# One-bank key groups, half-run query units and a ring of four load buffers in a fused attention and gated-convolution kernel

## The chip, the cores and the metric

The kernel runs on one core of one Trainium2 chip. The metric is the device time of one execution in microseconds (us); lower is better.

## The reference

Linear attention with a Hedgehog feature map, followed by a gated linear unit whose gate is a causal convolution. B = 8 batches, H = 8 heads, 576 tokens, head width 64, 128 features, model width 512.

```python
def phi(x):
    proj = np.einsum('bhsd,df->bhsf', x, w_phi)
    proj = proj - np.max(np.abs(proj), axis=-1, keepdims=True)
    return np.concatenate([np.exp(proj), np.exp(-proj)], axis=-1)
q_p, k_p = (phi(q), phi(k))
kv = np.einsum('bhsf,bhsd->bhfd', k_p, v)
z = np.sum(k_p, axis=2)
num = np.einsum('bhsf,bhfd->bhsd', q_p, kv)
den = np.einsum('bhsf,bhf->bhs', q_p, z)[..., None] + 1e-06
x = (num / den)                       # then heads are joined: B, S, 512
# gated unit, K = 5 taps
for k in range(K):
    gate_pre += conv_w[k][None, None, :] * xp[:, k:k + S, :]
gate = 1.0 / (1.0 + np.exp(-gate_pre))
out = (gate * (x @ w_val)) @ w_out
```

## The kernel before

The work is written as some 1,060 tasks, made by `build` and carried out by `Emit`. Each task has an engine and a place in the string ORDER, which was written out ahead of time; `Plan.follow` reads it, so every engine's instructions stand in the program in that order and each engine runs its own in sequence. FLEX names the engine (A ScalarE, D VectorE, P GpSimd) of each task that has a choice, and BANKS the PSUM banks of each group. There are eight banks, and a bank is used again only when everything that reads its group is done. WARM and ZERO place matmuls that compute nothing (zeros added to a group, or a product that nobody reads) at given places of the order.

A batch goes through these steps. All of k and q of a batch are 18 blocks of 128 columns, cut into `UNITS`: four units of four blocks and one of two.

- Loads. Batch 0 comes in float32 through SyncE's queue (`load32`), is transposed on TensorE (`tp32`) and copied out by `tc32`. Batches 1 to 7 come through GpSimd's queue as bf16 (`load`), from batch 2 on into two buffers KQN, one for k and one for q, and are transposed by DMA from SyncE's queue (`xpose`). `hold` and `holdx` are small GpSimd copies that hold later loads back until an earlier transfer is done.
- Keys. `kp` projects a unit into two PSUM banks (one for each half of the rows), VectorE takes the maxima over both banks at once (`kmax`, line 585), ScalarE the two exponentials, each over both banks (`kexp`, line 595). `ek` takes the exponentials of the maxima, `vs` multiplies v by them on GpSimd (line 610), and `st` sums the products of keys and values on TensorE (line 620); `kv` copies them out.
- Queries. `qm` projects and `qmax` takes maxima; the maxima are transposed (`mqt`), negated (`mqr`) and spread by `rx` (line 682); `qp` projects again and adds them in PSUM (lines 693 and 698), and `qexp` takes the exponentials (lines 706 and 709). In the units of `qp` the four blocks of a unit lie in both runs k of a head's columns of QTIL, a quarter of each.
- Numerators. `num` (line 719, and 726 for the remainder) waits for all query exponentials of the batch; `nrm` divides; the result is transposed on TensorE (`xtp`, line 748) and copied (`xtc`), or, for the batches in XB, transposed by DMA (`xtd`, line 755).
- Gated unit. `gate` (line 781), `tanh` (line 785), `val` (line 791), `gv` (line 797), `out` (lines 813 and 817), `oev` and the stores `odma`.

The order runs several batches at once: the keys of batch b+2 stand beside the queries of batch b+1 and the gated unit of batch b.

## Time and profile before

| | before |
|---|---|
| median of 3 runs | 218.91 us (218.59 to 219.14) |
| profiled execution | span 217.7 us; its own time is listed as no other figure, and the median lies 1.2 us above the span |
| busy: TensorE, ScalarE, VectorE, GpSimd | 195.5, 180.8, 170.2, 132.8 us |
| instructions | 9029 |
| DMA | 39.92 MB, mean 183 GB/s |

A group's row gives its line, engine and operation, what it writes and reads with its shape, the count, the busy time in us and the mean of one in ns, and then the idle time just before its instructions and what ended it. In the chain and in the order of time a row is start, duration, engine, line and how many instructions were merged. A bracket at the end is the idle time before it and its releaser. PEld is the loading of weights into TensorE, PEclk its granted clock.

### The profile page before, as it was taken

The page shows a single profiled execution, that of the slowest core. Times are in us where ns is not written, and L with a number is a line of the kernel's source. Part 1 is how long each engine was busy: PE and PEld are TensorE (multiplying, and loading weights), DVE is VectorE, ACT ScalarE, POOL GpSimd, SP SyncE. Part 2 cuts the span into 40 slices and gives each one's busy share as a digit, 9 for nine tenths or more (in the row PEclk, how much of TensorE's full clock was granted, in tenths as well). Part 3 has the DMA queues.
Part 4 walks back from the last instruction along what each step waited for, and adds up shares of the span by engine and source line. Part 5 has one row for each costly group of instructions (what it writes and reads, how often), then busy time and mean ns, then how long its engine had stood idle before and what let it go on. Part 6 is the DMA issues. An engine that isn't in the chain of part 4 may idle for free.

```text
span 217.7 us, 9029 instructions
## 1 busy us (share of the span) xinstructions
PE 195.5 (90%) x3946; PEld 138.6 (64%) x3946; DVE 170.2 (78%) x257; ACT 180.8 (83%) x267; POOL 132.8 (61%) x172
## 2 busy tenths in 40 slices
PE   2787887778999999998999999999999999899990
PEld 2555565566676676676857776567757766687740
DVE  3199979999789988997899978998699897654510
ACT  3589999999989899998999997999988988634251
POOL 3055999897793838970999089902993879210010
PEclk9999999999999999999999999999999999999997
DMA  6999998899899799989999778969953265764166
GB/s 177 364 234 215 302 188 231 149 174 199 144 152 284 139 135 213 302 154 174 233 276 168 88 165 248 190 142 203 287 183 89 63 160 128 81 168 97 48 186 202
DMA packets 49954, 39.92 MB, mean 183 GB/s; under 512 B 34165, under 2 KB 39541, under 8 KB 49914
## 3 DMA queue, kind: packets, MB, share of 16 engines
q1 hardware_dynamic: 43616, 28.65, 55.6%
q0 software_dynamic: 6032, 10.49, 26.3%
q8 instruction: 31, 0.51, 0.9%
q10 hardware_dynamic: 266, 0.21, 0.3%
q14 instruction: 9, 0.07, 0.1%
HBM read 30.48 MB, written 9.44 MB: 183 GB/s over the span
## 4 chain that ended last, share of the span: by engine, by line
PE 52%; ACT 23%; DVE 14%; DMA 5%; issue 4%; SPq 0%; DVEq 0%; ACTq 0%
PE PS L791 11%; ACT QTIL L706 9%; PE PS L781 9%; PE PS L813 9%; ACT KTIL L595 8%; DVE MQP L585 5%; PE PS L620 5%; PE PS L577 4%; PE PS L719 4%; DVE MK L585 3%; DMA KTIL<-in_k_dram 3%; PE PS L693 2%; DMA XT<-XN 2%; PE PS L817 2%; PE PS L698 2%
## 5 line engine op out<-in xcount | busy, mean ns | idle before, releaser
L595 ACT ACTIVATE KTIL<-PS 128x1024 bf16<-128x1024 f32 (+1 forms) x80 | 71.9, 960 | 4.1 <-PE PS L577 2.0
L610 POOL TENSOR_TENSOR VT<-VN,EK 128x1152 bf16<-128x1152 f32 x32 | 67.9, 2123 | 4.0 <-ACT EK L604 3.9
L706 ACT ACTIVATE QTIL<-PS 128x1024 bf16<-128x1024 f32 x64 | 62.5, 1044 | 2.4 <-PE PS L698 1.6
L682 POOL TENSOR_TENSOR RX<-MQR,ident 128x512 bf16<-128x512 bf16 (+1 forms) x39 | 36.6, 964 | 35.7 <-DVE MQR L670 26.0
L585 DVE TENSOR_REDUCE MK<-PS 128x8 f32<-128x1024 f32 (+1 forms) x40 | 44.2, 1112 | 2.9 <-PE PS L577 1.2
L585 DVE TENSOR_REDUCE MQP<-PS 128x8 bf16<-128x1024 f32 (+1 forms) x40 | 43.6, 1112 | 3.1 <-PE PS L577 2.3
L791 PE MATMUL PS<-XT,WV 128*128 128x288 bf16 x256 | 34.8, 286 | 0.3 <-DVE GV L797 0.2
L797 DVE SCALAR_TENSOR_TENSOR GV<-TH,PS 128x576 bf16<-128x576 bf16 x32 | 23.8, 752 | 10.4 <-PE PS L791 4.7
L813 PE MATMUL PS<-WOUT,GV 128*128 128x512 bf16 x128 | 31.3, 380 | 0.0
L791 PEld LDWEIGHTS <-WV 128*128 128x128 bf16 x256 | 23.8, 98 | 7.9 <-issue 1.4
L785 ACT ACTIVATE TH<-PS 128x576 bf16<-128x576 f32 x32 | 20.3, 663 | 9.5 <-PE PS L781 6.3
L620 PE MATMUL PS<-VT,KTIL 64*128 64x65 bf16 x1152 | 23.3, 191 | 1.1 <-issue 1.0
L781 PE MATMUL PS<-XT,GW 64*64 64x288 bf16 x640 | 23.1, 285 | 0.9 <-DMA XT<-XN 0.8
L740 DVE TENSOR_TENSOR XN<-PS,RCP 128x512 bf16<-128x512 f32 x32 | 22.1, 692 | 1.5 <-DMA XT<-XN 0.4
L620 PEld LDWEIGHTS <-KTIL 64*128 64x128 bf16 x1152 | 20.8, 94 | 3.8 <-issue 2.5
L719 PEld LDWEIGHTS <-QTIL 128*128 128x128 bf16 x512 | 18.3, 97 | 6.4 <-issue 4.0
L719 PE MATMUL PS<-KV,QTIL 128*128 128x65 bf16 x512 | 20.3, 194 | 0.3 <-DVE MQP L585 0.2
L781 PEld LDWEIGHTS <-GW 64*64 64x64 bf16 x640 | 17.8, 106 | 3.3 <-DVE RCP L737 0.9
L634 ACT ACTIVATE OUTS<-PS 128x512 f32<-128x512 f32 x22 | 13.5, 619 | 7.3 <-PE PS L813 6.1
L577 PE MATMUL PS<-W,qT 64*128 64x128 bf16 x288 | 15.1, 217 | 3.7 <-ACT qT L544 0.9
L813 PEld LDWEIGHTS <-GV 128*128 128x128 bf16 x128 | 11.1, 98 | 11.3 <-issue 0.6
L577 PEld LDWEIGHTS <-qT 64*128 64x128 bf16 x288 | 10.6, 94 | 10.3 <-issue 5.2
(79 smaller groups left out, 235.6 us busy)
## 6 DMA issues: line engine op xcount, KB each, us to landing
out_dram<-OUTS SPq DMA_DIRECT2D x32, 256.0 KB, 3.4
VN<-in_v_dram SPq DMA_DIRECT2D x7, 1152.0 KB, 6.3
KQN<-in_q_dram POOLq DMA_DIRECT2D x6, 576.0 KB, 8.3
KQN<-in_k_dram POOLq DMA_DIRECT2D x6, 576.0 KB, 9.8
KTIL<-in_k_dram SPq DMA_DIRECT2D x4, 288.0 KB, 4.5
VN<-in_v_dram POOLq DMA_DIRECT2D x1, 1152.0 KB, 10.6
KTIL<-in_q_dram SPq DMA_DIRECT2D x4, 256.0 KB, 5.7
out_dram<-OUTS SPq DMA_DIRECT2D x14, 64.0 KB, 2.6
```

The costliest lines, as they stand in the source:

```text
L577: nc.tensor.matmul(self.PS[:, t.grp.banks[par], i * P:(i + 1) * P], X[rows, (c0 + i) * P:(c0 + i + 1) * P], self.W2[rows, :], start=True, ...
L585: self.nc.vector.tensor_reduce(o, self.two(t.grp, n * P).rearrange("p a (c f) -> p a c f", f=F), AX.X, ALU.max, apply_absolute_value=True)
L595: self.nc.scalar.activation(self.KTIL[b % 2][:, s, c0:c0 + n, :, :].rearrange("p c a f -> p a c f"), self.two(t.grp, n * P).rearrange("p a ...
L610: nc.gpsimd.tensor_tensor(self.VT[g][:, s, :, 0:D], self.VN[b % 2][:, NC * g:NC * g + NC, :], e.to_broadcast([P, NC, D]), ALU.mult)
L620: nc.tensor.matmul(self.PS[:, t.grp.banks[ab], (s * 2 + x) * E1:(s * 2 + x + 1) * E1], self.KTIL[b % 2][rows, s, J // 2, J % 2, :], self.V ...
L682: self.nc.gpsimd.tensor_tensor(o, *wide(self.MQR[self.mq(b, u)][:, :], self.ident2), ALU.mult)
L706: self.nc.scalar.activation(o, i, AF.Exp, scale=1.0 - 2.0 * s)
L719: nc.tensor.matmul(self.PS[:, t.grp.banks[h // 4], (h % 4) * E1:(h % 4 + 1) * E1], Q[:, s, c % 2, h, (c // 2) * P:(c // 2 + 1) * P], self. ...
L781: self.nc.tensor.matmul(self.PS[o * D:(o + 1) * D, t.grp.banks[par], 0:R], self.GW[r, jj, 4 - m, :], X[r, 4 * a + jj, :, HALO - 8 * s:HALO ...
L791: self.nc.tensor.matmul(self.PS[:, t.grp.banks[par], 0:R], self.WV[:, i, (2 * j + par) * D:(2 * j + par + 2) * D], X[:, 4 * par + i, :, HA ...
L797: nc.vector.scalar_tensor_tensor(out=self.GV[b % 3][:, j, :, :], in0=self.TH[j][:, :, :], scalar=1.0, in1=self.two(t.grp, R), op0=ALU.add, ...
L813: nc.tensor.matmul(self.PS[:, t.grp.banks[0], :], GV[:, j, c % 2, (c // 2) * XH:(c // 2) * XH + P], self.WOUT[:, j, c % 2, :], start=(j == ...
```

## The change

Several things change at once, and ORDER, FLEX and BANKS are written anew (1,179 tasks).

- A key unit's two banks become two groups of one bank. `kp` still fills both; `kmax` and `kexp` work on one bank each, so there are twice as many of them at half the width, and each bank comes free by itself.
- `qp` units 0 to 3 now hold half of one run each: eight blocks' worth of rows, of one of the two runs. `num` c waits only for the two units of its run (or the remainder's one). `rx`, RX and the maxima follow that layout.
- Four KQN buffers in a ring; k is loaded before q; a load waits only for the transposition that read its buffer, and `holdx` is no longer called. GV has two buffers instead of three, OUTS six instead of eight.
- XB grows from batches 6 and 7 to 4, 5, 6 and 7.
- `rx` in all batches and `vs` may run on VectorE as well. By the new FLEX three `rx` (one before) and two `vs` (none before) do; ScalarE has 5 of batch 0's copies (9 before), 2 `kv` (4), 2 `xtc` (5) and 21 `oev` (22).
- w_phi comes in one DMA instead of two, the convolution weights through SyncE's queue. WARM and ZERO give 7 and 24 matmuls (6 and 152 before).

```diff
--- before.py
+++ after.py
-XB = (6, 7)
+QOF = {(0, 1): (0, 2), (2, 3, 4): (1, 3, 4), (0, 1, 2, 3, 4): (0, 1, 2, 3, 4)}
+QNEED = ((0, 1), (2, 3), (0, 1), (2, 3), (4,))
+XB = (4, 5, 6, 7)
 HOLDU = 4
-NO = 8
+NO = 6
+NK = 4
 NJ = 2 * NC
...
-WARM = (
-    "60:6:1 81:1:1 87:7:2 134:7:1 141:7:1 "
-)
-ZERO = "35:76:7 61:80:5 75:34:1 101:105:1 118:99:1 126:215:8 144:223:1 155:192:4 158:200:1 175:315:6 189:346:1 195:241:2 197:241:2 211:327:1"
+WARM = "97:7:4 111:2:2 277:6:1"
+ZERO = "171:215:6"
...
-                    hold = [None, A("lk", b, 0, "POOL", 0.15, fn("hold", HOLDU), [lds[HOLDU]], rank=-600)]
+                    hold = [None, A("lk", b, 0, "POOL", 0.15, fn("hold", HOLDU), lds + klds, rank=-600)]
+                else:
+                    klds = lds
...
-                hx = A("lk", b, 0, "POOL", 0.15, fn("holdx", b - 1), [G("xq", b - 1, 0)])
-                first = [hx]
+                first = [h["lk", b - 1]]
...
-            for w in "qk":
-                ld = A("l" + w, b, 0, "POOL", 0.75, fn("load", w, b), first, rank=-500 + (w == "k") if b == 1 else None, lat=0.6)
+            for w in "kq":
+                war = []
+                if b >= 2:
+                    n = 2 * b + "kq".index(w) - NK
+                    war = [G("x" + "kq"[n % 2], n // 2, 0)] if n >= 4 else []
+                ld = A("l" + w, b, 0, "POOL", 0.75, fn("load", w, b), first + war, rank=-500 + (w == "k") if b == 1 else None, lat=0.6)
                 xf[w] = A("l" + w, b, 0, "DMA", 4.2 if w == "k" else 3.9, None, [ld])
                 first = [ld]
+            h["lk", b] = ld
...
-                x = A("x" + w, b, 0, "SP", 2.7, fn("xpose", w, b), last + dp, lat=-1.5)
-                last = [x]
+                x = A("x" + w, b, 0, "SP", 2.7, fn("xpose", w, b), [xf[w]] + dp, lat=-1.5)
...
-            cc = A("mqt", 0, 0, "PE", 0.5, fn("c_cw"), [G("tp", "q", 1)], g, rank=-500)
+            cl = A("lk", 0, 0, "SP", 0.5, fn("c_cwl"), [])
+            cl = A("lk", 0, 0, "DMA", 3.0, None, [cl])
+            cc = A("mqt", 0, 0, "PE", 0.5, fn("c_cw"), [G("tp", "q", 1), cl], g, rank=-500)
...
         for u, (c0, n) in enumerate(UNITS):
-            g = plan.group("kp", 2)
-            kp = h["kp", b, u] = A("kp", b, u, "PE", 0.057 * n, fn("kp", b, u), [G("xk", b, u)], g, 1)
-            h["kmax", b, u] = A("kmax", b, u, "DVE", dve(2 * n * P, 0.08), fn("kmax", b, u), [kp, G("ek", b - 2)], g)
-            for s in range(2):
-                h["kexp", b, u, s] = A("kexp", b, u, "ACT", act(2 * n * P), fn("kexp", b, u, s),
-                                       [kp] + [G("st", b - 2, i, x) for i in range(2) for x in range(2)]
-                                       + ([G("tp", w, i) for i in range(NU) for w in "kq"] if b == 1 else []), g)
+            gs = [plan.group("kp", 1) for _ in range(2)]
+            kp = h["kp", b, u] = A("kp", b, u, "PE", 0.057 * n, fn("kp", b, u), [G("xk", b, u)], gs[0], 1, also=gs[1])
+            for a in range(2):
+                h["kmax", b, u, a] = A("kmax", b, u, "DVE", dve(n * P, 0.08), fn("kmax", b, u, a), [kp, G("ek", b - 2)], gs[a])
+                for s in range(2):
+                    h["kexp", b, u, s, a] = A("kexp", b, u, "ACT", act(n * P), fn("kexp", b, u, s, a),
+                                              [kp] + [G("st", b - 2, i, x) for i in range(2) for x in range(2)]
+                                              + ([G("tp", w, i) for i in range(NU) for w in "kq"] if b == 1 else []), gs[a])
...
-                h["vs", b, gi, s] = A("vs", b, gi, "POOL", 2.22, fn("vs", b, gi, s),
+                h["vs", b, gi, s] = A("vs", b, gi, ("POOL", "DVE"), (2.22, 1.36), fn("vs", b, gi, s),
                                       [eks[gi % len(eks)], G("lv", b)] + [G("st", b - 1, gi, x) for x in range(2)])
...
-            for u in us:
+            for u in QOF[us]:
                 n = UNITS[u][1]
-                h["rx", b, u] = A("rx", b, u, ("POOL", "DVE") if b == 0 else "POOL", (0.35 * n - 0.1, dve(n * P)) if b == 0 else 0.35 * n - 0.1,
+                h["rx", b, u] = A("rx", b, u, ("POOL", "DVE"), (0.35 * n - 0.1, dve(n * P)),
                                   fn("rx", b, u, i), [mqr, G("qp", b - 1, u)], gm if b == 0 else None)
...
-            qp = h["qp", b, u] = A("qp", b, u, "PE", 0.118 * n, fn("qp", b, u), [rx, G("xq", b, u)], g, 1)
+            qp = h["qp", b, u] = A("qp", b, u, "PE", 0.118 * n, fn("qp", b, u), [rx] + [G("xq", b, y) for y in QNEED[u]], g, 1)
...
-        allq = [G("qexp", b, u, s) for u in range(NU) for s in range(2)] + [G("kv", b, i) for i in range(2)]
         for c in range(5):
             g = plan.group("num", 2 if c < 4 else 1)
-            num = h["num", b, c] = A("num", b, c, "PE", 0.57 if c < 4 else 0.38, fn("num", b, c), allq,
+            need = [G("qexp", b, u, s) for u in ((2 * (c // 2), 2 * (c // 2) + 1) if c < 4 else (4,)) for s in range(2)]
+            num = h["num", b, c] = A("num", b, c, "PE", 0.57 if c < 4 else 0.38, fn("num", b, c), need + [G("kv", b, i) for i in range(2)],
...
-                              [h["tanh", b, j], vl] + [G("out", b - 3, c) for c in range(4)] + [G("gvc", b - 3)], g)
+                              [h["tanh", b, j], vl] + [G("out", b - 2, c) for c in range(4)] + [G("gvc", b - 2)], g)
...
-        bufs = TT("KQN", 2, [P, NC, 2 * D])
+        bufs = TT("KQN", NK, [P, NC, 2 * D])
         for b in range(2, B):
             for i, w in enumerate("kq"):
-                self.N[w][b] = bufs[i]
+                self.N[w][b] = bufs[(2 * b + i) % NK]
...
-        for i in range(2):
-            nc.scalar.dma_start(self.W32[i * D:(i + 1) * D, :], self.wphi[:, :])
+        nc.scalar.dma_start(self.W32[:, :], self.wphi[:, :].unsqueeze(0).to_broadcast([2, D, F]))
         nc.vector.tensor_copy(self.W2[:, :], self.W32[:, :])
-        nc.scalar.dma_start(self.cw5[:, :], self.wts[1][:, :])
+
+    def c_cwl(self, t):
+        self.nc.sync.dma_start(self.cw5[:, :], self.wts[1][:, :])
 
...
     def hold(self, t, u):
-        c = UNITS[u][0] * P
-        self.nc.gpsimd.tensor_copy(self.HOLD[:, :], self.XN32["q"][:, c:c + 1])
+        x = self.KTIL[1][:, :, :, :, :].rearrange("p s c a f -> p s (c a f)").bitcast(FP32)
+        self.nc.gpsimd.tensor_copy(self.HOLD[:, :, :], x.rearrange("p s (u x) -> p s u x", x=256)[:, :, :, 0])
...
+    def bank(self, t, par):
+        return t.grp.banks[par] if t.also is None else (t.grp, t.also)[par].banks[0]
...
-    def kmax(self, t, b, u):
+    def kps(self, t, n):
+        return self.PS[:, t.grp.banks[0], 0:n * P].rearrange("p (c f) -> p c f", f=F)
+
+    def kmax(self, t, b, u, a):
         c0, n = UNITS[u]
-        self.amax(t, self.MK[b % 2][:, c0:c0 + n, :].rearrange("p c a -> p a c"), n)
-
-    def kexp(self, t, b, u, s):
+        self.nc.vector.tensor_reduce(self.MK[b % 2][:, c0:c0 + n, a], self.kps(t, n), AX.X, ALU.max, apply_absolute_value=True)
+
+    def kexp(self, t, b, u, s, a):
         c0, n = UNITS[u]
-        self.nc.scalar.activation(
-            self.KTIL[b % 2][:, s, c0:c0 + n, :, :].rearrange("p c a f -> p a c f"),
-            self.two(t.grp, n * P).rearrange("p a (c f) -> p a c f", f=F),
-            AF.Exp, scale=1.0 - 2.0 * s)
+        self.nc.scalar.activation(self.KTIL[b % 2][:, s, c0:c0 + n, a, :], self.kps(t, n), AF.Exp, scale=1.0 - 2.0 * s)
 
...
-            nc.gpsimd.tensor_tensor(self.VT[g][:, s, :, 0:D], self.VN[b % 2][:, NC * g:NC * g + NC, :], e.to_broadcast([P, NC, D]), ALU.mult)
-            nc.gpsimd.tensor_copy(self.VT[g][:, s, :, D:E1], e)
+            eng = nc.gpsimd if t.eng == "POOL" else nc.vector
+            eng.tensor_tensor(self.VT[g][:, s, :, 0:D], self.VN[b % 2][:, NC * g:NC * g + NC, :], e.to_broadcast([P, NC, D]), ALU.mult)
+            eng.tensor_copy(self.VT[g][:, s, :, D:E1], e)
...
     def rx(self, t, b, u, i):
-        c0, n = UNITS[u]
+        y0, ny = self.qys(u)
+        nh = H if u < 4 else 2 * H
 
         def wide(m, e):
-            return (m.rearrange("p (h x) -> p h x", h=2 * H).unsqueeze(2).to_broadcast([P, 2 * H, n, 8]),
-                    e[:, c0:c0 + n].unsqueeze(1).unsqueeze(3).to_broadcast([P, 2 * H, n, 8]))
-
-        o = self.RX[u][:, :, 0:n, :]
+            m = m.rearrange("p (h k x) -> p h k x", h=H, k=2)[:, :, u // 2, :] if u < 4 else m.rearrange("p (h x) -> p h x", h=2 * H)
+            return (m.unsqueeze(2).to_broadcast([P, nh, ny, 8]),
+                    e[:, y0:y0 + ny].unsqueeze(1).unsqueeze(3).to_broadcast([P, nh, ny, 8]))
+
+        o = self.RX[u][:, 0:nh * ny * 8].rearrange("p (h y x) -> p h y x", h=nh, y=ny)
+        mq = self.mq(b, 2 if u in (1, 3) else 0 if u < 4 else 4)
         if t.eng == "POOL":
-            self.nc.gpsimd.tensor_tensor(o, *wide(self.MQR[self.mq(b, u)][:, :], self.ident2), ALU.mult)
-        else:
-            with self.nc.allow_low_precision("bf16 maxima"):
+            self.nc.gpsimd.tensor_tensor(o, *wide(self.MQR[mq][:, :], self.ident2), ALU.mult)
+            return
+        with self.nc.allow_low_precision("bf16 maxima"):
+            if b == 0:
                 self.nc.vector.tensor_tensor(o, *wide(self.PS[:, t.grp.banks[0], :].bitcast(BF16)[:, 0:P], self.nident2), ALU.mult)
+            else:
+                self.nc.vector.tensor_tensor(o, *wide(self.MQR[mq][:, :], self.ident2), ALU.mult)
+
+    def qys(self, u):
+        return (8 * (u % 2), 8) if u < 4 else UNITS[4]
 
     def qp(self, t, b, u):
         nc = self.nc
-        c0, n = UNITS[u]
+        y0, ny = self.qys(u)
+        w = UNITS[u][1] * P
...
-            nc.tensor.matmul(self.PS[:, t.grp.banks[par], 0:n * P], self.W2[rows, :],
-                             X[rows, c0 * P:(c0 + n) * P].rearrange("p (y h x) -> p h y x", y=n, h=2 * H),
+            m = X[rows, y0 * P:(y0 + ny) * P]
+            m = m.rearrange("p (y h k x) -> p h k y x", y=ny, h=H, k=2)[:, :, u // 2] if u < 4 else m.rearrange("p (y h x) -> p h y x", y=ny, h=2 * H)
+            nc.tensor.matmul(self.PS[:, t.grp.banks[par], 0:w], self.W2[rows, :], m,
                              start=True, stop=True, skip_group_check=True)
...
-            o = self.QTIL[b % 2][:, s, :, :, :].rearrange("p a h (k r) -> p a (h k) r", k=2)[:, :, :, u * 32:(u + 1) * 32]
-            self.nc.scalar.activation(o, i, AF.Exp, scale=1.0 - 2.0 * s)
+            self.nc.scalar.activation(self.QTIL[b % 2][:, s, :, :, u * D:(u + 1) * D],
+                                      self.two(t.grp, n * P).rearrange("p a (h r) -> p a h r", h=H), AF.Exp, scale=1.0 - 2.0 * s)
...
-        GV = self.GV[b % 3]
+        GV = self.GV[b % 2]
```

45 lines of the change are left out of this document (22 added, 23 removed), and 77 rows, old and new, of the table ORDER.

## The prediction

> **What bounds the kernel now.** The page comes first: its span, its busy shares, its slices and its chain.
>
> ```profile
> span 217.7 us, 9029 instructions
> ...
> PE 195.5 (90%) x3946; PEld 138.6 (64%) x3946; DVE 170.2 (78%) x257; ACT 180.8 (83%) x267; POOL 132.8 (61%) x172
> ...
> PE   2787887778999999998999999999999999899990
> DVE  3199979999789988997899978998699897654510
> ACT  3589999999989899998999997999988988634251
> ...
> PE 52%; ACT 23%; DVE 14%; DMA 5%; issue 4%; SPq 0%; DVEq 0%; ACTq 0%
> ```
>
> The span is 217.7 us; the median of the three timed runs is 218.91, so 1.2 us lie around the span, and every sum below is made against the span. TensorE is busy for 90%, yet its digits are 7 and 8 in the first ten slices and 9 almost everywhere behind. ScalarE and VectorE show the reverse: at 9 from the third slice on, falling off only at the end. The chain says the same: TensorE carries 52% of it, ScalarE 23% and VectorE 14%. So there are two stages, and the view of windows separates them.
>
> ```profile
> core 0: us, PE busy (x) PEld busy (x) DVE busy (x) ACT busy (x) POOL busy (x), PEclk, DMA share, GB/s
> 0.00:10.00 10.00, 4.93 (x32) 3.83 (x33) 2.00 (x6) 3.83 (x5) 1.78 (x12) 1.00 0.82 258
> 10.00:20.00 10.00, 7.73 (x122) 5.60 (x121) 9.32 (x10) 9.34 (x15) 5.68 (x8) 1.00 1.08 244
> 20.00:30.00 10.00, 8.39 (x136) 5.49 (x137) 8.45 (x15) 9.28 (x18) 8.13 (x7) 1.00 1.09 244
> 30.00:40.00 10.00, 8.45 (x272) 6.57 (x271) 9.57 (x12) 9.60 (x13) 9.19 (x12) 1.00 0.93 214
> 40.00:50.00 10.00, 7.38 (x202) 5.88 (x197) 8.94 (x16) 9.78 (x13) 9.97 (x10) 1.00 0.96 166
> 50.00:60.00 10.00, 9.28 (x225) 6.42 (x223) 8.46 (x12) 9.46 (x16) 7.12 (x10) 1.00 0.95 170
> 180.00:190.00 10.00, 9.61 (x266) 6.93 (x266) 6.94 (x16) 7.58 (x12) 6.12 (x8) 1.00 0.63 92
> ```
>
> From 10 to 50 us ScalarE is busy 38.0 of 40 us and VectorE 36.3, while TensorE has 32.0, part of it filler (below). There the exponentials and maxima set the pace, and TensorE waits for PSUM banks. From 50 us on TensorE is at 9.28 of 10 and more, and it stays there to the end. A change can therefore gain in three places: by getting through the first 50 us sooner, by taking matmuls away behind them, and by closing the gaps of the last 30 us. What it adds to ScalarE or VectorE costs most in the first stage.
>
> **The change part by part.** The groups with their shapes kept apart, and the order of the first 54 us, price the pieces.
>
> ```profile
> L595 ACT ACTIVATE KTIL<-PS 128x1024 bf16<-128x1024 f32 x64 | 63.5, 1050 | 2.6 <-DVE MK L585 1.3 <-PE PS L577 0.6 <-DVE GV L797 0.3
> L595 ACT ACTIVATE KTIL<-PS 128x512 bf16<-128x512 f32 x16 | 8.8, 602 | 1.5 <-PE PS L577 1.3
> L585 DVE TENSOR_REDUCE MK<-PS 128x8 f32<-128x1024 f32 x32 | 38.9, 1219 | 2.3 <-PE PS L577 1.2 <-ACT KTIL L595 0.7 <-ACT KV L632 0.2
> L585 DVE TENSOR_REDUCE MK<-PS 128x4 f32<-128x512 f32 x8 | 5.5, 686 | 0.7 <-ACT KTIL L595 0.3 <-PE PS L504 0.3
> L610 POOL TENSOR_TENSOR VT<-VN,EK 128x1152 bf16<-128x1152 f32 x32 | 67.9, 2123 | 4.0 <-ACT EK L604 3.9
> L632 ACT CAST KV<-PS 128x520 bf16<-128x520 f32 x4 | 2.5, 625 | 0.0
> L632 ACT COPY XT<-PS 128x1024 bf16<-128x1024 bf16 x2 | 2.1, 1043 | 0.0
> L504 PE MATMUL PS<-ONES,NIL 64*128 64x128 bf16 x140 | 5.6, 216 | 0.0
> ```
>
> ```profile
> 7.29 0.90 PE L536 MATMUL PS<-ident_f,KTIL 128*128 128x128 f32 x3 [1.21 <-DMA KTIL<-in_k_dram]
> 8.13 1.04 PE L577 MATMUL PS<-W,kT 64*128 64x128 bf16 x16
> 9.21 1.94 ACT L595 ACTIVATE KTIL<-PS 128x1024 bf16<-128x1024 f32 x2 [0.39 <-PE PS L577]
> 10.32 0.69 DVE L542 CAST qT<-PS 128x512 bf16<-128x512 f32 x1 [4.80 <-ACT KTIL L595]
> 10.93 2.35 DVE L585 TENSOR_REDUCE MK<-PS 128x8 f32<-128x1024 f32 x2
> 18.49 1.09 ACT L595 ACTIVATE KTIL<-PS 128x512 bf16<-128x512 f32 x2
> 28.23 0.63 PE L577 MATMUL PS<-W,qT 64*128 64x128 bf16 x16
> 53.85 1.28 ACT L785 ACTIVATE TH<-PS 128x576 bf16<-128x576 f32 x2
> ```
>
> *Splitting the key units.* Each batch has four units of 1024 columns and one of 512; each becomes two one-bank halves. So 40 maxima become 80 on VectorE and 80 exponentials become 160 on ScalarE. A pair of 1024-wide exponentials takes 1.94 from the first start to the last end; less one duration of 1.05 the second starts 0.89 after the first. A pair of 512-wide ones takes 1.09, less 0.60 is 0.49. Two halves cost 0.98 against 0.89: 0.09 per split, 80 x 0.09 = 7.2 us on ScalarE. From the means alone it would be 2 x 0.602 - 1.050 = 0.154 per split, 12.3 us; that is the upper bound, and zero the lower one, if the halves start while the other bank is still being filled or reduced. I take 0.09, because ScalarE runs these operations back to back in the crowded stages. On VectorE a pair of 1024-wide maxima takes 2.35, so the second starts 1.13 behind the first; a half takes 0.69, and with the same overlap of 0.09 0.60: 0.07 per split, 2.8 us in all.
>
> The errata section of the Trainium skill's page "VectorE: DVE Perf Modes" speaks against this part: it charges ScalarE 172 cycles per instruction that reads PSUM, and asks for tiles of 512 elements or more. At the 1.2 GHz it gives that is an estimated 0.143 per split, close to the upper bound and 11.5 us in all; the pair of halves at 18.49, 0.49 apart, does not bear that out for operations that follow one another.
>
> *Work moved between engines.* Decoding the letters of FLEX against the tasks: ScalarE loses 4 of its 9 first-batch copies, 2 of its 4 KV copies, one 1024-wide and two narrow XT copies and one output copy. At 0.49 per half-width operation, 0.9 for the wide one and 0.3 for a narrow one that is 7 x 0.49 + 0.9 + 0.6 = 4.9 us. VectorE takes the copies (4 + 2 + 1, at 0.60: 4.2), two of the 32 VT products and a net two of the RX products. No row shows a VT product on VectorE. GpSimd's 2.12 is the upper bound; the maxima's slope, (1219 - 686) / 512 = 1.04 ns per column, gives 1.2 plus overhead as the lower one. I take 1.5 with its small copy, since the slope is VectorE's own: 3.0; the RX products at the half's 0.60: 1.2. With the splits VectorE gains 2.8 + 4.2 + 3.0 + 1.2 = 11.2 us, XT copies left at nothing because it gets as many as it loses but for one.
>
> *The first stage.* Before, the third key transposition stood ahead of the first projection, waited 1.21 us for its load, and with that projection at 8.13 the first exponential came at 9.21. The new order has two key transpositions, a small query unit and then the projection. The wait of 1.21 and the 0.84 from 7.29 to 8.13 go; the small query load, now first on SyncE, gives back some 0.4: -1.7. VectorE, idle for 4.80 us until 10.32, now starts with the first copies. From the first exponential to the first tanh (53.85) ScalarE has two copies fewer (-1.0) and 26 splits (+2.3). That is -0.4 by ScalarE's work alone. Of its idle time, 2.0 us in 10 to 50, half closes, I estimate, since a numerator now needs only its own half of the query exponentials and VectorE is ahead: together -1.5. Bounds: -3.5 with its idle time all gone and splits at 0.05, +1.0 with none gone and VectorE late (its 4.80 us cover 2.4 of copies and 26 x 0.07 of splits, so there is room of 0.6 only).
>
> *Behind it.* XB sends the transpositions of batches 4 and 5 through DMA as well: four groups of TensorE transpositions less. The chain shows what one costs.
>
> ```profile
> 157.88 0.45 PE PS L748 x8
> 177.72 0.49 PE PS L719 x16
> 185.71 4.54 DMA XT<-XN
> 190.38 2.03 PE PS L781 x60
> 212.61 0.60 ACT OUTS L634
> ```
>
> 4 x 0.45 = -1.8 us of matmul time in the stage that TensorE bounds (0 where ScalarE has the end). Against it ScalarE has the other 54 splits, +4.9, less the 2.9 of KV, XT and output copies: +2.0. TensorE carries more than twice the chain that ScalarE does, so I put half of it on the path: +1.0. Bounds 0 and +3.1, that is all of it and 8 us of VectorE's additions at its 14% of the chain.
>
> *The end.* Gate matmuls of batch 6 begin at 190.38, when their DMA transposition has landed 4.54 us after the last normalization allowed it; from there TensorE is never out of work, and the last output copy begins at 212.61. The order of time gives TensorE's wait for it:
>
> ```profile
> 190.38 2.03 PE L781 MATMUL PS<-XT,GW 64*64 64x288 bf16 x60 [0.77 <-DMA XT<-XN]
> ```
>
> The new order puts two numerators (0.49 each) that stood behind that point ahead of it, and three output units of batch 5 there as cover. -0.8, bounds -1.8 (the two numerators and the wait) and +0.4. The last store is a whole 256 KB one:
>
> ```profile
> XT<-XN SPq DMA_TRANSPOSE x4, 3.8
> out_dram<-OUTS SPq DMA_DIRECT2D x32, 256.0 KB, 3.4
> ```
>
> Its 3.4 after an issue comes to what lies between 213.2 (212.61 + 0.60) and 217.7 now, so the tail of the tail stays.
>
> *Loads.* The ring of four lets k and q loads go ahead, and the copies that held GpSimd back are gone. The queue's own waits show what that is worth:
>
> ```profile
> SPq L565 <- DMA KQN<-in_k_dram: 49.8, 5, 19.7
> ```
>
> SyncE stood 49.8 us waiting for these loads, but the chain has no such load behind the first batch. This removes a wait that nobody waits for: 0. What I name as its cover is the order of SyncE's queue: stores and DMA transpositions stand behind those waits (rival two). GV falls to two buffers, OUTS to six: the products of batch b wait for the outputs of b-2, which stand ahead in TensorE's own order: 0. The convolution weights' load moves from ScalarE's queue to SyncE's, behind the first kT transposition; its reader stands behind the first numerators: 0, and up to +0.5 if SyncE is late. The run halves of the query units change patterns, not counts: 0.
>
> Sum: -1.5 - 1.8 - 0.8 + 1.0 = -3.1, so a span of 214.6 and, with 1.2 around it, **215.8 us**.
>
> **Rivals.** *One: the fixed cost per instruction wins.* Place: ScalarE, in both stages. If a split costs the 0.154 of the means, the first stage becomes +0.2 and the second 54 x 0.154 - 2.9 = +5.4, with ScalarE and no longer TensorE at the end of most waits, so that the 1.8 of transpositions is hidden: 0.2 + 5.4 - 0.8 = +4.8 if all of it is exposed, +2 if half is: 221 to 223.7, I say 222. It decides from about 0.15 per split on (3.1 / (26 + 27) above 0.09). For it: ScalarE at 9.3 to 9.8 of 10 in the first windows. Against: the spacing of 0.49. The errata rule quoted above would put the kernel just below that point, at about 218.6.
>
> *Two: the DMA transpositions of batches 4 and 5 arrive late.* Place: SyncE's queue, where they stand behind the kT transposition of batch 7, which waits for a load that GpSimd sends only after batch 5's RX products. One exposed transposition costs what the chain shows, 4.54, so 220.3. Against it: between the last numerator of batch 4 and its gate matmuls the order has four state, five numerator, four output, two value units, fifteen in all; each at no less than the 0.45 of the shortest row shown, that is 6.8 us at the least, against 4.54. It decides when SyncE reaches them more than 2.3 us late; the 49.8 us of waits say that SyncE can be late.
>
> *Three: nothing moves.* The first stage's gain is eaten by splits and the rest by an order that is tight elsewhere: 218.6 to 219.3, say 218.9.
>
> *Four: the clock.* The tables ZERO and WARM give 158 filler matmuls before and 31 after; the 5.6 us of L504 nearly vanish. In the first 10 us 16 projections took 1.04, at 28.23 0.63, though PEclk says 1.00 of both windows. If a quarter of the 26 us of real matmul time in 10 to 50 fell back to the first pace, 4.2 us more, three of them uncovered: 218.8 to 219. The Trainium skill's page "TensorE: Matmul & The Clock Gate", part 1, says that an idle window of some 3.4 us halves the clock. TensorE's longest wait in the rows shown is 1.21, so by that rule the clock stays and the forecast with it.
>
> **How the numbers follow.** The forecast has 0.50; the same with the first stage at its good end and the end at -1.8 (211.5 to 213) 0.10; rival one 0.14, two 0.11, three 0.10, four 0.05. About 0.3% (0.66 us) is what can be told from no change here. Faster by more than that: 0.60; within it: 0.10; slower: 0.30. The range leaves out the far ends of the good case and of rival one: 211.5 to 221.5. The likely side alone, the forecast with its bounds on the fast side, is 212.5 to 217.8.
>
> **What would show it.** Right: first exponential near 7.5 us; first tanh near 52; 512-wide KTIL exponentials about 0.49 apart; the group of XN transpositions down by 32 matmuls, with four more XT DMA transpositions; TensorE at 9 from the ninth slice; gate matmuls of batch 6 near 187. Wrong: halves 0.55 or more apart, or ScalarE at 10 of 10 with TensorE below 9 in the middle (one); idle time ahead of the gate group released by XT<-XN (two); a granted clock below 1 or 16 projections in 1 us after 10 us (four); a first tanh after 54 us would take my largest term away.

## The result and the profile after

The changed kernel takes 235.41 us (median of 4 runs, 234.2 to 240.32) where the kernel before took 218.88: a ratio of 1.0739 (95% interval 1.0687 to 1.0791), 16.2 us more. The forecast was 215.8. Ratios here and below leave out the runs that took over 1.5% more than the fastest of the same kernel. The page of the profiled run (235.77 us):

```profile
span 234.0 us, 8798 instructions
...
PE 198.8 (85%) x3770; PEld 138.0 (59%) x3787; DVE 180.8 (77%) x309; ACT 181.9 (78%) x337; POOL 127.2 (54%) x161
...
PE   2898698699999789869996999998699959799991
...
PEclk9999959999999999999999999999689999999999
...
q8 instruction: 29, 0.48, 0.8%
...
PE 56%; DVE 21%; DMA 9%; issue 6%; ACT 5%; POOL 1%; SPq 0%; DVEq 0%; POOLq 0%; ACTq 0%
```

TensorE's unbroken row of nines is gone: there are holes in the middle, and in two places the granted clock falls. DMA went from 5% of the chain to 9%, "issue" (time in which the engine waited for nothing that the profile shows) from 4% to 6%. The windows show part of the first stage and the two worst stretches:

```profile
core 0: us, PE busy (x) PEld busy (x) DVE busy (x) ACT busy (x) POOL busy (x), PEclk, DMA share, GB/s
...
30.00:40.00 10.00, 9.19 (x250) 7.78 (x247) 8.27 (x14) 9.60 (x20) 7.69 (x11) 0.73 0.99 143
40.00:50.00 10.00, 7.51 (x192) 6.01 (x186) 9.59 (x21) 9.71 (x18) 10.00 (x11) 1.00 1.17 194
50.00:60.00 10.00, 9.47 (x250) 6.88 (x244) 8.89 (x15) 9.53 (x20) 8.35 (x10) 1.00 1.14 157
160.00:170.00 10.00, 6.82 (x77) 3.99 (x69) 5.24 (x9) 4.17 (x9) 8.37 (x10) 0.75 0.86 209
180.00:190.00 10.00, 7.30 (x198) 5.40 (x198) 8.16 (x14) 7.30 (x12) 5.63 (x9) 1.00 0.77 245
```

In 160 to 170 us TensorE is idle for about a third of the time, VectorE and ScalarE for about a half: something outside them is late. TensorE's order of time has the five large holes behind the first stage (the bracket is the idle time before the row):

```profile
80.24 0.84 PE L638 MATMUL PS<-VT,KTIL 64*128 64x65 bf16 x42 [1.65 <-issue]
103.84 0.23 PE L638 MATMUL PS<-VT,KTIL 64*128 64x65 bf16 x4 [1.97 <-issue]
128.10 0.43 PE L810 MATMUL PS<-XT,GW 64*64 64x288 bf16 x6 [1.81 <-issue]
165.96 2.08 PE L820 MATMUL PS<-XT,WV 128*128 128x288 bf16 x8 [3.13 <-DVE OUTS L648]
189.76 0.82 PE L842 MATMUL PS<-WOUT,GV 128*128 128x512 bf16 x3 [2.70 <-issue]
```

Four of the five are "issue". The fourth has a named cause, VectorE's output copy, which itself waited for a store:

```profile
DVE OUTS L648 <- DMA out_dram<-OUTS: 3.9, 1, 3.9
...
PE PS L820 <- DVE OUTS L648: 3.1, 1, 3.1
```

The holes come to 11.3 us. Behind the fourth the clock was at half for 6.83 us (the trace's clock records: 165.07 to 171.90). TensorE ran again from 165.96, so this is worth at most 3.0 us of matmul time. Together that is 14.2 of the 16.3 us between the spans; whether each hole is lost time the sum doesn't say, the runs below do. Where the loss arises is seen when TensorE's work (columns streamed, a float32 one counted four times, without fillers and without the transpositions of XN) is laid against time (us), worked out from the matmuls of the traces. In the two profiles of the changed kernel 16 of the 128 matmuls of the output line have no record; they are counted in evenly with the rest of their line:

```
share done    before   changed   changed with few loads (below)
0.20           62.4      61.5      61.4
0.40          103.6     107.5     102.8
0.60          141.0     148.6     142.9
0.80          176.4     192.4     179.0
1.00          212.5     228.9     215.5
```

The changed kernel leads by 0.9 us at some 60 us and loses all of its time behind.

**What the "issue" holes are.** The page has a DMA queue of its own for instructions: q8, 29 packets, 0.48 MB, so 16 KB each. TensorE has 7,574 recorded instructions in this program, some 261 for each packet; a piece is taken here as 256 instructions, which the shifts of runs 5 to 7 test. The trace's DMA records give the start of each packet. Beside those of the four holes stand the large loads in flight (first and last packet, same records) and how many of TensorE's recorded instructions had run when it stopped, less 256 for each fetch made before:

```
fetch starts   large load in flight      hole at    instructions used up
 77.80         v, 74.2 to 78.2            78.6       440
101.40         v, 96.9 to 101.3          101.9       437
125.84         q, 122.4 to 125.8         126.3       436
187.52         v, 183.2 to 187.7         187.1       427
```

Each of the four fetches begins within some 0.4 us of the end of a load that has held the DMA engines for 3.4 to 4.5 us; TensorE goes on some 1.4 us after the packet has landed. 17 of TensorE's 7,574 records are missing in this trace; in the first experiment's, which has them all, the counts at its four such holes are 442, 442, 442 and 440. The earliest fetches in these traces start at a count of some 160. So TensorE can run to a count of 442, could be served from about 160 on, and stops when the fetch is late. Ahead of each of the four holes it ran groups of its short instructions, the 65-column states. Not every fetch waits for a load's end: those at 70.50, 83.53 and 137.31 began inside a load of q or k, at counts of 275, 345 and 238, and made no hole. In the kernel before the latest fetch starts at a count of 343, at 47.04, so TensorE never runs out there.

### The profile page after: what moved, and what is told of

Read it like the earlier page. It is cut to its first block, busy times and chain, and to the rows that moved or that the text cites. A ratio compares the mean times of both kernels' runs of the same rounds, so it can differ in the third digit from the quotient of the medians.

```text
span 234.0 us, 8798 instructions
## 1 busy us (share of the span) xinstructions
PE 198.8 (85%) x3770; PEld 138.0 (59%) x3787; DVE 180.8 (77%) x309; ACT 181.9 (78%) x337; POOL 127.2 (54%) x161
## 4 chain that ended last, share of the span: by engine, by line
PE 56%; DVE 21%; DMA 9%; issue 6%; ACT 5%; POOL 1%; SPq 0%; DVEq 0%; POOLq 0%; ACTq 0%
PE PS L820 11%; PE PS L842 11%; PE PS L810 7%; PE PS L591 6%; DVE MQP L602 6%; PE PS L638 6%; DVE MK L611 5%; PE PS L748 5%; DMA qT<-KQN 4%; DVE XN L769 3%; DMA out_dram<-OUTS 3%; PE PS L723 2%; DMA KTIL<-in_k_dram 2%; PE PS L846 2%; ACT KTIL L615 2%
## 5 line engine op out<-in xcount | busy, mean ns | idle before, releaser
L615 ACT ACTIVATE KTIL<-PS 128x512 bf16<-128x512 f32 (+1 forms) x160 | 80.4, 580 | 10.7 <-DVE MK L611 6.2
L628 POOL TENSOR_TENSOR VT<-VN,EK 128x1152 bf16<-128x1152 f32 x30 | 63.5, 2118 | 29.9 <-ACT EK L621 22.4
L733 ACT ACTIVATE QTIL<-PS 128x1024 bf16<-128x1024 f32 x64 | 64.6, 1043 | 5.3 <-PE PS L727 5.2
L611 DVE TENSOR_REDUCE MK<-PS 128x4 f32<-128x512 f32 (+1 forms) x80 | 48.3, 627 | 3.7 <-PE PS L591 2.3
L703 POOL TENSOR_TENSOR RX<-MQR,ident 128x512 bf16<-128x512 bf16 (+1 forms) x37 | 35.2, 973 | 26.6 <-DVE MQR L688 21.7
L820 PE MATMUL PS<-XT,WV 128*128 128x288 bf16 x256 | 36.1, 291 | 3.9 <-DVE OUTS L648 3.1
L842 PE MATMUL PS<-WOUT,GV 128*128 128x512 bf16 x112 | 30.2, 380 | 3.8 <-issue 3.2
L638 PEld LDWEIGHTS <-KTIL 64*128 64x128 bf16 x1152 | 21.8, 97 | 8.8 <-issue 4.8
L810 PE MATMUL PS<-XT,GW 64*64 64x288 bf16 x640 | 24.4, 290 | 2.0 <-issue 1.8
L652 ACT ACTIVATE OUTS<-PS 128x512 f32<-128x512 f32 x21 | 13.0, 619 | 15.1 <-PE PS L842 11.5
L591 PE MATMUL PS<-W,qT 64*128 64x128 bf16 x288 | 16.6, 230 | 3.9 <-DVE MQP L602 1.1
```

The source lines that it names most:

```text
L591: nc.tensor.matmul(self.PS[:, self.bank(t, par), i * P:(i + 1) * P], X[rows, (c0 + i) * P:(c0 + i + 1) * P], self.W2[rows, :], start=True, ...
L611: self.nc.vector.tensor_reduce(self.MK[b % 2][:, c0:c0 + n, a], self.kps(t, n), AX.X, ALU.max, apply_absolute_value=True)
L615: self.nc.scalar.activation(self.KTIL[b % 2][:, s, c0:c0 + n, a, :], self.kps(t, n), AF.Exp, scale=1.0 - 2.0 * s)
L628: eng.tensor_tensor(self.VT[g][:, s, :, 0:D], self.VN[b % 2][:, NC * g:NC * g + NC, :], e.to_broadcast([P, NC, D]), ALU.mult)
L638: nc.tensor.matmul(self.PS[:, t.grp.banks[ab], (s * 2 + x) * E1:(s * 2 + x + 1) * E1], self.KTIL[b % 2][rows, s, J // 2, J % 2, :], self.V ...
L703: self.nc.gpsimd.tensor_tensor(o, *wide(self.MQR[mq][:, :], self.ident2), ALU.mult)
```

## The experiments

The first four runs still had another theory: the store ring. The changes are against the changed kernel unless "before" is said. Ratios are against the kernel before, run on the same chip, and the time beside a ratio is the ratio times 218.9 us. Some profiles of the shifted kernels lack some of TensorE's records too.

**1. OUTS as a ring of eight.** (Start-up tiles lie on it so that it fits.)

```diff
-NO = 6
+NO = 8
```

> The changed kernel with OUTS as a ring of eight again instead of six, nothing else moved. Theory (store ring): the wait of 3.90 us of VectorE at 165.22 for a store from six output units earlier goes, and with it TensorE's idle 3.13 us at 162.83 and the 6.83 us of half clock behind it, which cost some 3.4 us of matmul time. So 7.3 us less than 235.4: 228, or 226 if later stores were late too. Rival (price of the halves, or the order itself): the store was only the last of several things that were late at that point, another wait of about the same length takes its place, and the time stays within 1.5 us of 235. Rival (queue): the store goes, but the gate matmuls of a later batch then wait for XT, and half comes back, 231 to 232.

Ratio 1.0836 (1.0725 to 1.0946): nothing gained. The store wait is gone, and a transposition of XN is late in its place; the "issue" holes stay:

```profile
PE PS L810 <- DMA XT<-XN: 2.6, 1, 2.6
```

```profile
189.78 1.46 PE L842 MATMUL PS<-WOUT,GV 128*128 128x512 bf16 x3 [2.73 <-issue]
```

The theory fell. Around 160 us both the store and the transposition were late, behind the load of v for batch 6 (in the changed kernel its packets run from 157.1 to 161.0); the ring only chose which one was met first.

**2. XT of batches 4 and 5 on TensorE.** 

```diff
 def xtd(self, t, b, i):
+    if b in (4, 5): (8 transpositions into a free bank, one copy); return
```

> The changed kernel with the transpositions of XN of batches 4 and 5 on TensorE again (32 matmuls, two copies on VectorE and two on ScalarE, in banks that are free at those places); the ring stays at six. Theory (store ring made late by SyncE's queue): the store of output unit (2,1) no longer stands behind two DMA transpositions, lands some 2 to 4 us sooner, and most of VectorE's wait of 3.90 us and of the half clock behind it goes: minus 7 us, plus 1.8 us for the matmuls, 230. If the ring alone is to blame and the queue is not: 235 + 1.8 = 237. Rival (price of the halves): 236 to 237.

1.0695 (1.058 to 1.081), 234: not told from the changed kernel. In its profile VectorE no longer waits for a store, and the holes of 3.13 and 2.70 are gone, but those behind the first stage that are "issue" are 2.48, 2.10 and 2.33. The edit also adds 64 instructions, an estimated 1.8 us of matmuls (4 x 0.45). So what the transpositions themselves do to the stores isn't separated from the moved pieces here.

**3. More filler in the first stage.**

```diff
-ZERO = "171:215:6"
+ZERO = "133:229:3 136:255:3 141:114:2 144:249:3 148:253:5 153:247:3 155:117:2 171:215:6"
```

> The changed kernel with some 100 more filler matmuls (adding zeros into open units) between 25 and 30 us, where TensorE waits for VectorE. Theory (store ring): the stretch of half clock from 28.5 to 35.3 us goes; it lay in the stage that ScalarE and VectorE bound, so it was worth at most 1.5 us, and the end stays late: 234 to 235.5. Rival (clock): lost filler is what made the change slow, both stretches of half clock go (6.8 us of lost matmul time) and the time falls to 229 or less.

1.0454 (1.0358 to 1.0549): 229, over 6 us gained, and the clock at 1.0 throughout. That fits the rival on the clock; but most of the gain arises behind 148 us (at 0.60 of TensorE's work the run is 2.2 us ahead of the changed kernel, at the end 7.5), over 100 us behind the fillers, and the first tanh stayed where it was (52.3 for 52.0). The fillers had also put 152 more instructions into TensorE's stream. That led to the fetches.

**4. Whole key units in the new order.**

```diff
 def kexp(self, t, b, u, s, a):      # kmax likewise
+    both banks at the first of the two halves, nothing at the second
```

> The changed kernel with both halves of each key unit joined again in one exponential and one maximum, as before the change, at the place of the first of the two halves: 80 fewer instructions on ScalarE, 40 fewer on VectorE, banks freed as late as the second half frees them. Theory (store ring): 80 x 0.09 us less on ScalarE, of which little is on the path; the late store stays: 233 to 236. Rival (price of the halves): at 0.154 us each on ScalarE and 0.07 on VectorE, 12.3 and 2.8 us come back, most of it exposed: 224 to 228.

1.2045 (1.1952 to 1.2138), 264: far worse, against both theories. The order lets ScalarE and VectorE work on different banks of one unit; with whole units they wait for each other:

```profile
ACT KTIL L628 <- DVE MK L622: 18.8, 18, 1.8
DVE MK L622 <- ACT KTIL L628: 15.2, 15, 2.4
```

So this run doesn't price a split; run 11 does.

**5 to 7. Shifting TensorE's stream by 64, 128 and 256 instructions.**

```diff
+for _ in range(32):          # 64, 128
+    nc.tensor.matmul(em.PS[:, 7, 0:32], em.ONES[:, 0:P], em.ONES[:, 0:32], start=True, stop=True)
 for i, t in enumerate(plan.follow()):
```

> The changed kernel with 32 tiny matmuls (32 columns of ones into a bank that is free) ahead of TensorE's first instruction, where it waits for its first load anyway: 64 more instructions in its stream, no dependence touched. New theory (instruction fetch): TensorE's instructions come by DMA in pieces of 16 KB, 256 instructions; a fetch that becomes due while a large load holds the DMA engines begins only when that load has ended, and TensorE stands still when it has used up the 442 instructions that it holds. The stalls of 1.65, 1.97, 1.81, 3.13 and 2.70 us at 78.6, 101.9, 126.3, 162.8 and 187.1 and the 6.8 us of half clock behind the fourth are those. 64 instructions earlier the pieces end in other places: the stalls change their places and sizes, and the time moves by several us, most likely down, to 226 to 233. Rival (clock in the first stage, filler): the filler at 25 to 30 us of the experiment before is what gave 7 us, this one leaves that stage as it was, 234 to 236. Rival (order and waits): 234 to 236.

> The same with 64 tiny matmuls, 128 instructions, half a piece. Instruction fetch: the stalls of the changed kernel fall elsewhere, 224 to 232, and the time differs by more than 2 us from at least one of the other two shifts. Rivals (clock by filler, order and waits): 234 to 236 for all three shifts.

> The same with 128 tiny matmuls, 256 instructions: one whole piece, so that every later piece ends where it did in the changed kernel. Instruction fetch: stalls near 79, 102, 126, 163 and 187 again, give or take what the start loses to the matmuls, 234 to 238. Rival (filler of any kind keeps the clock up): this has most of it and is the fastest of the three, below 230.

64: 1.0735 (1.0654 to 1.0815), as the changed kernel; 128: 1.0396 (1.0278 to 1.0513), 227.6, over 7 us less; 256: 1.0766 (1.0675 to 1.0856), back again. All four runs of the half-piece shift lie between 225.7 and 232.6, those of the whole one between 234.9 and 241.4. With the shift of one whole piece three of the four "issue" holes stand before the very instructions of the changed kernel, and the store's at 165 us too:

```profile
80.26 0.84 PE L638 MATMUL PS<-VT,KTIL 64*128 64x65 bf16 x42 [1.63 <-issue]
126.34 0.43 PE L810 MATMUL PS<-XT,GW 64*64 64x288 bf16 x6 [2.09 <-issue]
165.54 2.08 PE L820 MATMUL PS<-XT,WV 128*128 128x288 bf16 x8 [3.16 <-DVE OUTS L648]
189.53 0.82 PE L842 MATMUL PS<-WOUT,GV 128*128 128x512 bf16 x3 [2.98 <-issue]
```

The one at 102 is gone: this time its fetch started at 97.54, early in the load of v (96.8 to 101.7), and a hole of 0.80 stands one piece later, at 105.2. In the profile of the half-piece shift one "issue" hole of over 1.1 us is left (2.04, up to 82.27); a hole of 4.06 behind it, up to 91.62, is released by a transposition of q from KQN. The 64 were a miss: holes moved (2.97 us, up to 187.21, within a state group) but did not get smaller. The expectation was also wrong in counting the hole at 163 among the fetches: only 216 instructions had run there, it is the store's.

**8. No loads of v from batch 2 on.**

```diff
 def loadv(self, t, b):
+    if b >= 2: return
```

> The changed kernel without the loads of v for batches 2 to 7 (the old values in VN are used again), six loads of 1152 KB less, all else as it was. Instruction fetch: the fetches that started late behind these loads (77.8, 101.4, 187.5 us) start when they are due, and the stalls of 1.65, 1.97 and 2.70 us go, while the one at 126.3 behind a load of k or q stays: 6 to 10 us less, 225 to 229. Rival (order and waits): the loads of v are not on the chain, nothing changes: 234 to 236.

1.0213 (1.0128 to 1.0297), 223.6: 11.5 us less, though the chain has no load of v. The holes of 1.65 and 1.97 are gone, that of 2.70 is down to 0.85, and the store's of 3.13 and the half clock behind it are gone with them; the one behind the load of q is left:

```profile
PE PS L812 <- issue: 2.3, 1, 2.3
```

**9. The loads of v in quarters.**

```diff
-eng.dma_start(VN, rows("v", b))
+one quarter here, the others each behind a later step of SyncE
```

> The changed kernel with each load of v from batch 2 on cut into its four quarters of 288 KB; the first goes where the whole load went, each other one behind a later step of SyncE's queue. The bytes and the order of all else stay. Instruction fetch: a fetch waits for a quarter (some 1.2 us at the rate of the whole loads) and not for 4 to 5 us, so the stalls behind these loads (1.65, 1.97, 2.70 us) go as they did without the loads: 225 to 230. Rival (it is the bytes that slow kT, qT and XT transpositions down, not the fetches): 232 to 236.

1.0517 (1.0476 to 1.0557), 230.2: 4.9 us back with the same bytes, at the edge of the expectation. In its profile the largest "issue" holes behind the first stage are 1.78 (up to 106.58) and 1.18 (at the place of the 2.70); the store's is down to 1.44.

**10. The kernel before, shifted by 128 instructions.** (The same edit as 6.)

> The kernel before with 64 tiny matmuls, 128 instructions, ahead of TensorE's first instruction. Instruction fetch: its loads wait in turn for GpSimd's copies, so fetches are late by at most 5.3 us there; if only its phase was a lucky one, some stalls of 1 to 2 us appear and it takes 220 to 225; if pacing the loads is what keeps it clear, it stays at 218 to 220. Rivals that have nothing to do with fetches: 218.5 to 219.5.

1.0004 (0.9962 to 1.0047). One hole appears in its profile, 2.46 us at 52.4 (the fetch starts at a count of 441), and the time doesn't show it. So the kernel before is not clear of the holes by luck of phase alone. Its loads wait for GpSimd's copies of the batch before, and v, q and k of a batch follow one another once per batch. That this pacing is what spares it is argued from the traces: no run puts it back into the changed kernel.

**11. The kernel before with halves alone.**

```diff
 def kexp(self, t, b, u, s):         # kmax likewise
+    for a in range(2): one activation on bank a
```

> The kernel before with every key exponential and key maximum cut into its two one-bank halves, one right behind the other, and nothing else: 80 more instructions on ScalarE, 40 more on VectorE, none on TensorE. At 0.09 us per split on ScalarE, with the first stage paying all and half of the rest on the path: 26 x 0.09 + 0.5 x 54 x 0.09 = 4.8 us more, 223.7. Rival (the means' 0.154 per split, all on the path): up to 12 us more, 228 to 231. If the halves cost nothing where TensorE sets the end: 219 to 221.

1.0031 (0.9997 to 1.0065): +0.7 us, not the 4.8 expected. ScalarE's key exponentials rise from 72.3 us (63.5 + 8.8) to 78.6, by 0.079 per split, and nearly all of it is hidden:

```profile
L600 ACT ACTIVATE KTIL<-PS 128x512 bf16<-128x512 f32 x128 | 68.5, 673 | 1.5 <-PE PS L577 1.3 <-PE PS L504 0.2
L600 ACT ACTIVATE KTIL<-PS 128x256 bf16<-128x256 f32 x32 | 10.1, 435 | 1.4 <-PE PS L577 1.3
```

**12. The kernel before with XB = (4, 5, 6, 7) alone.**

```diff
 def xtp(self, t, b, i):
+    if i < 2 and b in (4, 5): return self.xtd(t, b, i)
 def xtc(self, t, b, i):
+    if i < 2 and b in (4, 5): return
```

> The kernel before with the transpositions of XN of batches 4 and 5 by DMA, at the places in the order where TensorE had them, and their copies gone: the changed kernel's XB alone. Forecast's term: 4 x 0.45 = 1.8 us less, 217.1, as long as the transpositions are covered. Rival (late DMA transpositions, and the stores behind them): 220 to 223. Instruction fetch: the stream is shorter by 64 instructions from batch 4 on, so the late pieces end elsewhere, which can give or take 2 us.

1.0235 (1.0185 to 1.0284): 5.1 us slower. In the chain one transposition takes not 4.54 but 14.52 us, and a gate group waits for it:

```profile
136.91 14.52 DMA XT<-XN
```

```profile
151.56 1.41 PE L785 MATMUL PS<-XT,GW 64*64 64x288 bf16 x20 [1.24 <-DMA XT<-XN]
```

The DMA records show packets of the loads of q and k of batch 7 from 135.8 to 148.2, through most of those 14.5 us. The hole ahead of it is the same thing from the other side, a normalization that may not write XN while a transposition still reads it:

```profile
148.55 0.69 DVE L740 TENSOR_TENSOR XN<-PS,RCP 128x512 bf16<-128x512 f32 x1 [2.37 <-DMA XT<-XN]
```

Half a clock for 3.41 us (from 151.09) follows.

**13. The fillers of 3 and a shift that makes both one whole piece.** (52 tiny matmuls ahead, 128 in all.)

> The changed kernel with the 76 more filler matmuls at 25 to 30 us that gave 7 us, and 52 tiny ones ahead of TensorE's first instruction: together 128, 256 instructions, one whole piece. Instruction fetch: behind the first stage every piece ends where it did in the changed kernel, the stalls near 79, 102, 126, 163 and 187 are back, 233 to 237. Rival (the fillers' gift is the clock held up from 28 to 35 us): 227 to 230 as before.

1.0703 (1.0627 to 1.0778), 234.3: the gain of run 3 is gone though its fillers are there and the clock is full through the first stage here too. What had gained was the moved stream, not that clock.

**14 and 15. Both kernels with few loads.**

```diff
 def loadv(self, t, b):
+    if b >= 2: return
 def load(self, t, w, b):
+    if b >= 4: return
```

> The changed kernel without the loads of v from batch 2 on and without those of k and q from batch 4 on (what lies in the buffers is used again): the stall of 2.28 us at 120 that was left without the loads of v, and its 3.4 us of half clock, go too. Instruction fetch: 219 to 221. If the order, the halves or the DMA transpositions cost something by themselves, it stays at 223 or more.

> The kernel before without the same loads, for comparison. Instruction fetch and pacing: its loads cost it little, 216 to 218.5, so that without loads the two kernels are 1 to 4 us apart and not 16. Rival (loads slow both alike, the difference is the order's): the kernel before falls by as much as the changed one, to 207 or less.

Changed: 1.0145 (1.0105 to 1.0185), 222.1. Before: 1.0009 (0.9981 to 1.0037), unmoved. So 13 of the 16.2 us hang on the loads, and 3.0 are left (the two ratios' difference, 1.4%). The largest "issue" hole behind the first stage is 0.95 now, and the stretch at 160 that had 6.82 is full:

```profile
160.00:170.00 10.00, 9.90 (x137) 6.03 (x133) 8.95 (x14) 8.54 (x16) 1.95 (x4) 1.00 0.01 2
170.00:180.00 10.00, 9.05 (x239) 6.64 (x238) 8.77 (x16) 8.69 (x18) 6.67 (x10) 1.00 0.48 134
180.00:190.00 10.00, 8.25 (x211) 5.29 (x210) 8.27 (x14) 8.25 (x12) 7.06 (x8) 1.00 0.32 68
```

What is left of the loss arises behind some 100 us (the table of work against the kernel before: 0.8 ahead at 0.40, 1.9 behind at 0.60, 2.6 at 0.80, 3.0 at the end).

**16. Quartered loads of v, and XT of batches 4 and 5 on TensorE.** (2 and 9 together.)

> The changed kernel with the loads of v in quarters, and the transpositions of XN of batches 4 and 5 on TensorE (32 matmuls more). If the DMA transpositions cost time by sharing the engines with loads, some 2 to 4 us less than the quarters alone: 227 to 229. If only the fetches matter: 230.9 + 1.8 = 232.7, give or take 2 for the shift of the stream by 64 instructions.

1.0574 (1.0495 to 1.0653), 231.5, not told from run 9: no cost or gain of these transpositions by DMA can be told in the new order. This run too has 64 instructions more, so pieces end elsewhere.

**17. Without the one load of v of batch 7.**

```diff
+    if b == 7: return
```

> The changed kernel without the load of v of batch 7 alone (the values of batch 5 in that buffer are used again). Instruction fetch: nothing changes before 180 us, the stall of 2.70 us at 187 goes: 235.4 - 2.7 = 232.7. Rival (the order around that point is late anyway, the stall only shows it): another wait takes its place, 235.

1.064 (1.0556 to 1.0725), 232.9: the expected size, though the intervals overlap. In its profile the hole at 187 is gone.

**18. That one piece made due sooner.**

```diff
+    for _ in range(48 if i == 956 else 0): one tiny matmul into bank 2
```

> The changed kernel with 48 tiny matmuls (96 instructions, some 1.4 us of TensorE) ahead of the output unit at 179 us, into a free bank: the next piece is then due some 2 to 3 us sooner, before the load of v of batch 7 holds the engines. Instruction fetch: the stall at 187 goes or shrinks below 1 us though work was added: 235.4 - 2.7 + 1.4 = 234, and 1 to 3 us of shift in the later small stalls either way. Rival (order): 1.4 us more, 236.8, with the stall as it was.

1.0529 (1.0449 to 1.0609), 230.5, with 1.4 us of work added and no load taken away. The fetch now starts at 179.4, ahead of the load, and the group that was cut by 2.70 us runs through:

```profile
185.31 0.40 PE L591 MATMUL PS<-W,kT 64*128 64x128 bf16 x8
185.64 1.04 PE L842 MATMUL PS<-WOUT,GV 128*128 128x512 bf16 x4
```

It came out 3.5 us below the expectation. Other holes also fell out otherwise in it (1.38 one piece later in place of 1.97, but 3.61 for the store's 3.13, with 3.41 us of half clock behind it in place of 6.83), so its time alone isn't the price of this hole.

## Why the prediction was wrong

**The step that failed is "Loads": priced at 0** because no load stood on the chain and SyncE's 49.8 us of waits were nobody's. Those waits, and GpSimd's copies, had set when the loads ran. Sent ahead, the loads fill the DMA engines for 3 to 5 us at other moments, and what else goes by DMA is late: TensorE's own instructions, which neither the sum nor a rival names (8.1 us of holes), and a store or else a transposition of XN (3.1), which the sum puts at 0 beside loads. Through that last hole the clock falls (at most 3.0). Without most loads 13 us of the loss are gone, and the kernel before gains nothing from the same cut. Runs 8, 9 and 14 show it by taking loads away or apart, 7 and 13 by putting the pieces back where they were, 18 by moving one. Transpositions of q from KQN are late as well: one took 9.71 us of the chain up to 87.1, though TensorE waited only 0.92 for it. Why the waits of before kept loads and fetches apart is argued, not shown: its loads of v take 4.3 to 6.6 us behind the first stage, against 3.9 to 4.5 in the changed kernel.

**OUTS 8 to 6: priced at 0, with a reason that held for GV only.** The wait of 3.9 us is on that ring; but with eight buffers another late transfer took 2.6 us at the same place, so the ring costs nothing by itself (run 1).

**XN transpositions by DMA: -1.8 forecast, nothing won.** In the order of before they cost 5.1 us (run 12), in the new one nothing that can be told from the moved pieces (2, 16). Rival two had the mechanism, a late transposition, but put it down to SyncE's queue and priced it at the 4.54 us that the chain showed for batch 6. It was 14.5 beside two loads: the bound should have come from a place where loads run.

**The splits: +4.8 forecast, +0.7 (0.0 to 1.4) measured** (run 11). The forecast's terms hold 26 x 0.09 in the first stage and half of 54 x 0.09 behind it. The price of one was near (0.09 forecast, 0.079 measured); what failed is how much of it lies on the path. Six halves in a row in the changed kernel take 3.13 us, so (3.13 - 0.60) / 5 = 0.51 apart, where 0.49 was forecast:

```profile
17.47 3.13 ACT L615 ACTIVATE KTIL<-PS 128x512 bf16<-128x512 f32 x6
```

Rival one falls, and the charge of 172 cycles that the Trainium skill's page "VectorE: DVE Perf Modes" makes in its errata section (an estimated 0.143 us per split) isn't met by operations that follow one another here.

**The first stage: -1.5 forecast, -1.8 measured** at the first tanh. First exponential at 8.45 (7.5 forecast, 9.21 before), first tanh at 52.04 (52, and 53.85 before):

```profile
8.45 3.22 ACT L615 ACTIVATE KTIL<-PS 128x512 bf16<-128x512 f32 x6
...
52.04 0.72 ACT L814 ACTIVATE TH<-PS 128x576 bf16<-128x576 f32 x1
```

That the sum fits is partly luck: the first exponential came 0.76 sooner where 1.7 was forecast, and the 2.3 us of splits in the same sum are more than all of run 11 lost.

**Rival four, the clock,** was right that it would fall to half (28.5 to 35.3 us, and again at 165), wrong on the price of the first: the stage is ScalarE's and VectorE's, and the lead was there at the first tanh; run 13 has the full clock there and gains nothing. The prediction kept its forecast because the longest wait in its rows was 1.21 us; that step did not hold: in the 3.4 us ahead of 28.54 no wait that ended was over 0.42, but TensorE was busy for only 2.12 us (2.92 in run 13, where the clock stayed). Rival four had no word of the second fall.

**The end: -0.8 forecast.** No gain there was measured. With few loads 3.0 us are still lost, from some 100 us on. VectorE's VT product is one late item: priced at 1.5 each, one took 1.35, the other, beside GpSimd's own product, 3.31. TensorE's wait for it is 0.9; the rest of the 3.0 was not taken apart. (In the forecast's tail, a store of 3.4 does not fill the 4.5 us between 213.2 and 217.7; no term hung on it.)

**The range,** 211.5 to 221.5, did not hold the time. It was built from rivals that shared the forecast's list of what uses DMA. No run was faster than the kernel before; the best of the changed family that leaves nothing out is the half-piece shift at 1.0396.

## What to carry to other kernels

A load that nobody waits for is not free: ask what else goes by DMA while it runs, instruction fetches among them, and take "issue" idle time in the middle of a group of short matmuls as a sign to look at the instruction queue's packets beside the loads. Waits that pace loads can be worth keeping; if they are taken out, cut the loads or place them by hand. To test for late fetches, shift the engine's stream by half a piece and by a whole one: what moves with the first and comes back with the second is most likely a fetch. Look at the holes and not at the time alone: a shift by a quarter of a piece moved them here and left the time as it was.
